# Index lists, row gathers and weight loads of the second expert issued behind a transpose; six constant products ahead of the fold

## The chip, the core and the metric

The kernel runs on one core of one Trainium2 chip. The metric is device time in microseconds, the median of repeated runs. Engines in the text: TensorE (PE, matrix products; its weight loads are PEld), VectorE (DVE), ScalarE (ACT), GpSimd (POOL) and SyncE (SP). SP and POOL here mostly issue DMA transfers; SP issues in the order in which the program is written.

## The reference

Three stages in a row, all in float32.

1. A linear attention with decaying state: for each of 4 batches and 8 heads, 768 steps, `y[t] = r[t] (state + u k[t] v[t])`, then `state = w[t] state + k[t] v[t]`, head size 48.
2. A dense layer on the 3072 rows of 384 values: `h = (x w1 * x w2) w3`, then `x = h w_out` (1024 wide inside).
3. A mixture of 8 experts: a gate `x w_gate` with noise scaled by `log(1 + exp(x w_noise))`, the two highest experts of each row, a softmax over those two, and `out[rows of e] += weight * (max(x[rows of e] w1[e], 0) w2[e])`, 384 to 1024 to 384.

## The kernel before

Nearly every product is done as three products of a high part and a low part (`mm3`, lines 179 to 182: high by high, low by high, high by low), so TensorE's work stands in lines L180, L181 and L182 for all stages.

**Fold.** The first 50 us load `w3` and `w_out`, convert them, and multiply them together once (`mm_w3`), so that stage 2 needs one product less for each row. Lines 529 to 548 are the loop over 19 steps `u`: step `u` converts a piece, `mm_w3(u - 3)` uses the piece of three steps before, `wo_T(u)` transposes a piece of `w_out` on TensorE and `gate_cols(u - 1)` multiplies the piece transposed a step earlier by the gate's weights. `warm_up(n)` (lines 514 to 516) issues `n` products of a constant tile of ones, 128 by 512 in bf16, into a bank that nobody reads; each is pinned behind the TensorE instruction written before it. There are ten before the loop, and three at the end of steps 0 and 1.

**Middle.** Attention, the dense layer and the gate run interleaved from about 50 to 460 us, by a table of slots. The gate writes, for each expert, a list of row numbers and weights into a table in DRAM (`slots`).

**Experts.** An expert has room for 800 rows (CAP), as 7 pieces: pieces 0 to 3 of 128 rows (first half), pieces 4 and 5 of 128 and piece 6 of 32 rows (second half, 288 rows). For each expert the rows come this way:

- `load_idx`: SP loads the list of row numbers from the table (L800; L808 for the first expert).
- `gather`: POOL issues an indirect DMA for each piece, from the rows in DRAM to a tile `xg` (L848; L817 for the first expert).
- `store` (L854; L822 for the first expert): SP writes the piece back to DRAM, in order (`expert_rows`).
- `turn` / `turn_first` (L860, L829): SP issues a DMA transpose from there into `XTx`, which has to wait for the stores.
- `tr` (L865, L866): ACT and DVE make the high and the low part.
- `mm1(hf, ff)`: eight blocks of 9 products into the hidden layer, for one half of the rows. `mm2(e, j)`: the products of piece `j` with the second weights, after which ACT scales the result (L898) and POOL adds it to the output by an indirect DMA (L908).

An expert's weights come as two loads of 768 KB for the first matrix (`load_e(e, 0, i)`, tile `raww`, L781) and two for the second (`load_e(e, 1, i)`, tile `raw`); `split_e` makes their high and low parts (L788, L791).

What sets the order around the change: SP's loads, stores and transposes and the casts of `tr` and `split_e` on ACT are pinned in the order of the program. DVE's order is the program's. POOL's and most of TensorE's instructions are ordered by a planner that goes by its own estimate of when their inputs are there, ties in the order of the program. So SP is one line in which a waiting instruction holds up all behind it.

The first expert is handled apart (lines 1023 to 1072), since its last rows are known only when the gate has ended. The last two pieces of its rows, 5 and 6, are gathered while `mm2` of pieces 0 to 3 already runs (lines 1043 to 1056): after `mm2(0, 0)` come the second expert's first index list and gathers (`need(1, 0, 0)`), the stores of pieces 5 and 6, their transpose (`turn_first(NT - 2, CAP)`, 160 rows, called the late rows below) and the second expert's two first loads. `mm1(1, ff)` of the first expert needs that transpose. Behind its eight blocks the program writes `turn(1, 0)`, which stores and transposes the second expert's first 512 rows. `turn` has an argument `mid`, called between the stores and the transpose; it is used at line 1070 with `load_w2`.

Of the kernel before, what the change touches and what calls it, by code (L numbers as in the profile page):

```python
# [71 lines left out]
def tile_kernel(ctx: ExitStack, tc: tile.TileContext, dt, nat, w3t, wout, w1, w2, e1, e2, cf, ci, out):  # L72
# [63 lines left out]
    def split(h, l, src, on=None):  # L136
        act.copy(out=h, in_=src)
        (on or dve).tensor_tensor(out=l, in0=src, in1=f(h), op=OP.subtract)
# [20 lines left out]
    def flush(n=2):  # L159
        for _ in range(n):  # L160
            low, LQ[:] = LQ[:], []
            while CQ:
                mid, t, z, h, l, post = CQ.pop()
                dve.scalar_tensor_tensor(z, mid, 13, t, op0=OP.logical_shift_right, op1=OP.bitwise_or)
                x = z.bitcast(F32)
                act.copy(out=h, in_=x)
                LQ.append((h, l, x))
                if post:
                    post(x)
            for h, l, x in low:  # L170
                dve.tensor_tensor(out=l, in0=x, in1=f(h), op=OP.subtract)
# [215 lines left out]
    def ld_raw(n=1):  # L387
        for _ in range(n):
            if order:
                k, u = order.pop(0)  # L390
                rawx[k, u] = load64(raws.tile([P, 1026], I32, name="rawf"),
                                    wout[u] if k == "o" else w3t[u // 8, u % 8])

    def cv_wo(j):
        cvt(rawx["o", j], DM, woh[:, j, :DM], wol[:, j, :DM], post=lambda x: xo_.__setitem__(j, x))

    def wo_T(j):
        bank = PB[4 + j % 2]
        for kb in range(3):
            pe.transpose(bank[:, P * kb:P * kb + P], xo_[j][:, kb * P:kb * P + P], ident)  # L400
        xo_[j] = fold.tile([P, DM], F32, name="woT")
        act.copy(out=xo_[j], in_=bank[:, :DM])

    def gate_cols(j):
        g = bK[:, 256 + 32 * j:272 + 32 * j]
        for kb in range(3):
            pe.matmul(g, xo_[j][:, P * kb:P * kb + P], wgn[:, kb], start=kb == 0, stop=kb == 2)

    def gate_split(j):
        split(woh[:, j, DM:], wol[:, j, DM:], bK[:, 256 + 32 * j:272 + 32 * j])  # L410

    def cv_w3(u):
        w3s[u] = [fold.tile([P, 512], F32R, name=x, bufs=3) for x in ("w3h", "w3l")]
        cvt(rawx["3", u], 512, *w3s[u])

    def mm_w3(u):
        jb = u % 8
        for fb in range(4):
            s = slice(fb * P, fb * P + P)
            mm3(PB[fb][:, :XW], w3s[u][0][:, s], w3s[u][1][:, s], woh[:, jb, :], wol[:, jb, :], jb == 0, jb == 7,  # L420
                tc.keep_in_program_order if u == 15 else lambda x: x)
            if u == 7:
                split(W0[0][:, fb], W0[1][:, fb], PB[fb][:, :XW])
# [40 lines left out]
    def run_todo(lo, hi):  # L464
        for slot in sorted(x for x in todo if lo <= x < hi):
            for fn, a in todo.pop(slot):
                fn(*a)
# [46 lines left out]
    def warm_up(n):  # L514
        for _ in range(n):
            tc.keep_in_program_order(pe.matmul(PB[6], warm[:, :P], warm, start=True, stop=True))
# [12 lines left out]
    for u in range(19):  # L529
        if u < 8:  # L530
            cv_wo(u)
            ld_raw()
        if u < 16:
            cv_w3(u)
            ld_raw()
        elif u == 16:
            flush()
        if u > 2:
            mm_w3(u - 3)
        if 0 < u < 9:  # L540
            gate_cols(u - 1)
            gate_split(u - 1)
        if u < 8:
            wo_T(u)
        if u < 2:
            warm_up(3)
        act.on = u >= 15
        run_todo(u - 24, u - 23)
# [226 lines left out]
    def load_e(e, m, i):  # L775
        if m == 0 and e:
            rw = EP["b"].tile([P, 1536], F32, name="raww", bufs=2)
        else:
            rw = rawp.tile([P, 1538], F32, name="raw2", tag="raw64")[:, :1536]
        RW[e, m, i] = rw  # L780
        tc.keep_in_program_order(sp.dma_start(out=rw, in_=(e1, e2)[m][e, :, 1536 * i:1536 * i + 1536]))  # L781
# [11 lines left out]
    def load_idx(e, hf, r):  # L793
        TI[e, hf] = EP["a"].tile([P, (TA, TB + 1)[hf], 2], I32, name=f"ti{hf}", bufs=3)
        for o, n, w, j in (((0, TA, TPT, 0),), ((HOLD, TB, TPT, 0), (CAP - TPL, 1, TPL, TB)))[hf]:
            if isinstance(r, int):
                v = table[e * CAPT + r * CAP + o:e * CAPT + r * CAP + o + w * n]
            else:
                v = table[bass.ds(r * CAP + (e * CAPT + o), w * n)]
            tc.keep_in_program_order(sp.dma_start(out=TI[e, hf][:w, j:j + n].rearrange("p j t -> p (j t)"),  # L800
                                                  in_=v.rearrange("(p j) t -> p (j t)", p=w)))
# [18 lines left out]
    def store_first(j):  # L820
        w = rows_of(j)
        tc.keep_in_program_order(sp.dma_start(  # L822
            out=rows[0, 2 * TPT * j:2 * TPT * j + 2 * w].rearrange("(p t) d -> p (t d)", t=2), in_=XG[0, j][:w]))
# [15 lines left out]
    def rows_of(j):  # L839
        return TPT if j < NT - 1 else TPL  # L840
# [5 lines left out]
    def gather(e, j, rows=NROW):  # L846
        XG[e, j] = EP["b" if e else "a"].tile([P, 2 * DM], U16, name="xg", bufs=NXG)
        pool.indirect_dma_start(out=XG[e, j][:rows_of(j)], out_offset=None, in_=x2d[:rows],  # L848
                                in_offset=bass.IndirectOffsetOnAxis(ap=ti(e, j)[:, 0:1], axis=0))

    def turn(e, hf, mid=lambda: None):

        for j in range(TA) if hf == 0 else range(TA, NT):
            tc.keep_in_program_order(sp.dma_start(  # L854
                out=rows[e % 2, 2 * TPT * j:2 * TPT * j + 2 * rows_of(j)].rearrange("(p t) d -> p (t d)", t=2),
                in_=XG[e, j][:rows_of(j)]))
        mid()
        a = 2 * hf * NAB[0]
        s = slice(a, a + 2 * NAB[hf])
        tc.keep_in_program_order(sp.dma_start_transpose(out=XT["x", hf].bitcast(U16), in_=rows[e % 2, s]))  # L860
# [24 lines left out]
    def mm2(e, j, mid=None):  # L885
        hf, jj = divmod(j, TA)
        n, s = rows_of(j), slice(TPT * jj, TPT * jj + rows_of(j))
        MC[0] ^= 1
        bank = bX[MC[0]][:, :DM]
        y = EP["b"].tile([P, DM], F32, name="ye", bufs=9)  # L890
        wt = ti(e, j)[:, 1:2].bitcast(F32)
        if j < NT - 1:
            for ff in range(8):
                if mid and ff == 4:
                    mid()
                w = slice(ff * DM, ff * DM + DM)
                mm3(bank[:n], Hh[hf][:, ff, s], Hl[hf][:, ff, s], WBh[:, w], WBl[:, w], ff == 0, ff == 7)
            act.activation(out=y[:n], in_=bank[:n], func=AF.Copy, scale=wt)  # L898
        else:

            for ff in range(8):
                g = ff % 4
                pe.matmul(bank[n * g:n * g + n], HM[hf][:, ff], RW[e, 1, ff // 4][:, g * DM:g * DM + DM],  # L903
                          start=ff < 4, stop=ff > 3, tile_position=(0, n * g))
            act.activation(out=y[:n], in_=bank[:n], func=AF.Copy, scale=wt)
            for g in range(1, 4):
                dve.scalar_tensor_tensor(y[:n], bank[n * g:n * g + n], wt, y[:n], op0=OP.mult, op1=OP.add)
        ins = pool.indirect_dma_start(out=out, out_offset=bass.IndirectOffsetOnAxis(ap=ti(e, j)[:, 0:1], axis=0),  # L908
                                      in_=y[:n], in_offset=None, compute_op=OP.add).ins

        if j == 0 or AD[0] != e:
            AD[:] = [e]
        for p in AD[1:]:
            tc.declare_no_dep(ins, p, reason="an expert's rows differ")
        AD.append(ins)

    def need(e, hf, r, rows=NROW):
        load_idx(e, hf, r)
        for j in range(TA) if hf == 0 else range(TA, NT):
            gather(e, j, rows)  # L920
# [125 lines left out]
    for j in range(TA):  # L1046
        mm2(0, j)
        if j == 0:
            need(1, 0, 0)
            for jj in (NT - 2, NT - 1):  # L1050
                store_first(jj)
            turn_first(NT - 2, CAP)
            load_e(1, 0, 0)
            load_e(1, 0, 1)
        if j == TA - 2:
            tr(0, 1)
    need(1, 1, 0)

    def load_w2():
        load_e(1, 1, 0)  # L1060
# [1 line left out]

    for ff in range(8):
        mm1(1, ff)
    turn(1, 0)
    for i, j in enumerate((TA, NT - 1, *range(TA + 1, NT - 1))):
        mm2(0, j)
        split_e(1, 0, i)
# [132 lines left out]
```

## Time and profile before

| what | value |
|---|---|
| median of 3 runs | 903.72 us (902.86 to 906.01) |
| the profiled execution's own time | 909.49 us |
| its span, first to last instruction | 907.7 us |
| PE, PEld | 97%, 90% of the span busy |
| DVE, ACT, POOL | 54%, 48%, 27% |
| mean granted TensorE clock | 0.993 of full speed |
| DMA | 139.18 MB, mean 153 GB/s |
| chain that ended last | PE 41%; DMA 1%, of which the transposes into XTx are the largest part |

Engine shares are shares of the span in which the engine had an instruction running. The granted clock is 1.00 at 2.4 GHz and 0.50 at 1.2 GHz. The chain that ended last is followed back from the last instruction, at each step to what released it. DMA shares are the mean busy share of 16 DMA engines; overlapping packets can bring a stretch above 1.

### The profile page before, as it was taken

How to read it: one execution, taken by the hardware profiler on the slowest of the kernel's cores; microseconds unless marked ns; L12 is line 12 of the kernel's file. 1: busy time of each engine (PE TensorE's matmuls, PEld its weight loads, DVE VectorE, ACT ScalarE, POOL GpSimd, SP SyncE). 2: the span in 40 equal slices, each digit the busy share in tenths (PEclk: the TensorE clock that was granted, in tenths of full speed). 3: DMA queues.
4: the chain of work that ended last, by engine and by line, in shares of the span. 5: the costliest groups of instructions: out<-in, count | busy, mean ns of one | idle time of the engine just before them, and what ended most of it. 6: DMA issues, size and time to landing. Idle time of an engine off the chain costs nothing. (4 is left out here: it accounts for less than half of the span.)

```text
span 907.7 us, 17628 instructions
## 1 busy us (share of the span) xinstructions
PE 882.4 (97%) x7010; PEld 816.1 (90%) x7010; DVE 491.6 (54%) x1208; ACT 436.3 (48%) x883; POOL 242.9 (27%) x216
## 2 busy tenths in 40 slices
PE   8899999999999999999998999999999999999994
PEld 6789799999999999999988989899998989989894
DVE  5899766756666657655472453443434334353430
ACT  7787666555546547544552443433334343433320
POOL 1200010231231231132334443316061341603122
PEclk9999999999999999999999999999999999999997
DMA  9963479474575654515145986829276482934112
GB/s 352 409 232 129 130 99 262 130 196 142 144 216 139 178 134 128 146 44 167 36 114 108 256 249 173 204 73 222 62 214 143 133 213 65 229 76 108 18 21 38
DMA packets 123581, 139.18 MB, mean 153 GB/s; under 512 B 74592, under 2 KB 103264, under 8 KB 123488
## 3 DMA queue, kind: packets, MB, share of 16 engines
q1 hardware_dynamic: 99952, 109.58, 41.3%
q0 software_dynamic: 12160, 19.72, 11.2%
q10 hardware_dynamic: 11376, 8.65, 3.3%
q8 instruction: 57, 0.93, 0.4%
q14 instruction: 36, 0.29, 0.1%
HBM read 88.12 MB, written 36.04 MB: 137 GB/s over the span
## 5 line engine op out<-in xcount | busy, mean ns | idle before, releaser
L908 POOL DMA_INDIRECT out<-ye,ti x49 | 77.4, 1579 | 235.5 <-ACT ye L898 215.3
L180 PE MATMUL pb<-XTh,WAh 128*128 128x512 f32 (+1 forms) x384 | 134.2, 350 | 3.0 <-ACT XTh L865 2.3
L181 PE MATMUL pb<-XTl,WAh 128*128 128x512 f32 (+1 forms) x384 | 133.0, 347 | 0.0
L182 PE MATMUL pb<-XTh,WAl 128*128 128x512 f32 (+1 forms) x384 | 131.8, 347 | 0.0
L180 PE MATMUL pb<-WBh,HH 128*128 128x384 f32 x384 | 130.2, 339 | 0.0
L181 PE MATMUL pb<-WBl,HH 128*128 128x384 f32 x384 | 129.3, 337 | 0.0
L182 PE MATMUL pb<-WBh,HH 128*128 128x384 f32 x384 | 129.3, 337 | 0.0
L881 DVE SCALAR_TENSOR_TENSOR HH<-pb,HH 128x256 fp32r<-128x256 f32 (+1 forms) x128 | 71.3, 557 | 87.2 <-ACT HH L880 79.9
L880 ACT ACTIVATE HH<-pb 128x256 fp32r<-128x256 f32 (+1 forms) x128 | 62.8, 491 | 115.2 <-PE pb L182 108.2
L898 ACT ACTIVATE ye<-pb,ti 128x384 f32<-128x384 f32 x42 | 24.4, 581 | 134.0 <-PE pb L182 108.4
L725 POOL DMA_INDIRECT slots<-g_sc,g_si x48 | 51.9, 1081 | 136.9 <-DVE g_si L724 71.9
L180 PEld LDWEIGHTS pb<-XTh,WAh 128*128 128x128 f32 x384 | 72.7, 189 | 15.1 <-DVE HH L881 4.0
L180 PE MATMUL pb<-xh,WAh 128*128 128x256 f32 x288 | 82.0, 285 | 0.3 <-ACT xh L86 0.3
L180 PE MATMUL pb<-xh,WBh 128*128 128x256 f32 x288 | 81.5, 283 | 0.0
L181 PE MATMUL pb<-xl,WAh 128*128 128x256 f32 x288 | 81.0, 282 | 0.2 <-DVE xl L337 0.2
L181 PE MATMUL pb<-xl,WBh 128*128 128x256 f32 x288 | 81.0, 281 | 0.0
L182 PE MATMUL pb<-xh,WAl 128*128 128x256 f32 x288 | 81.0, 282 | 0.0
L182 PE MATMUL pb<-xh,WBl 128*128 128x256 f32 x288 | 81.0, 281 | 0.0
L181 PEld LDWEIGHTS pb<-XTl,WAh 128*128 128x128 f32 x384 | 72.8, 190 | 8.8 <-DVE XTl L866 0.3
L182 PEld LDWEIGHTS pb<-XTh,WAl 128*128 128x128 f32 x384 | 72.3, 189 | 8.8 <-DVE WAl L791 0.2
L180 PEld LDWEIGHTS pb<-WBh,HH 128*128 128x128 f32 x384 | 72.1, 188 | 5.0 <-ACT WAh L788 3.8
L241 POOL TENSOR_TENSOR rku<-nrk 128x384 f32<-128x384 f32 x21 | 21.6, 1028 | 198.7 <-DVE cc L248 83.5
(194 smaller groups left out, 2063.5 us busy)
## 6 DMA issues: line engine op xcount, KB each, us to landing
dtc<-dt SPq DMA_DIRECT2D x24, 772.0 KB
raw<-e SPq DMA_DIRECT2D x18, 768.0 KB
raww<-e SPq DMA_DIRECT2D x14, 768.0 KB
nrk<-nat SPq DMA_DIRECT2D x24, 384.0 KB
expert_rows<-xg SPq DMA_DIRECT2D x45, 192.0 KB
rawf<-w3t SPq DMA_DIRECT2D x16, 512.0 KB
nv<-nat SPq DMA_DIRECT2D x24, 256.0 KB
out<-zeros SPq DMA_DIRECT2D x9, 576.0 KB
```

Source lines behind the costliest of these rows:

```text
L180: pin(pe.matmul(o, wh, xh, start=start, stop=False))
L181: pe.matmul(o, wh, xl, start=False, stop=False)
L182: pe.matmul(o, wl, xh, start=False, stop=stop)
L241: on.tensor_tensor(out=t, in0=RK[j][:, :DM], in1=RK[j][:, DM:], op=OP.mult)
L725: ins = pool.indirect_dma_start(out=table, out_offset=bass.IndirectOffsetOnAxis(ap=si[:, i, k:k + 1], axis=0), in_=SC[:, i, k, :], in_offs ...
L880: act.activation(out=Hh[hf][:, ff], in_=bank[:, :n], func=AF.Relu)
L881: dve.scalar_tensor_tensor(Hl[hf][:, ff], bank[:, :n], 0.0, f(Hh[hf][:, ff]), op0=OP.max, op1=OP.subtract)
L898: act.activation(out=y[:n], in_=bank[:n], func=AF.Copy, scale=wt)
L908: ins = pool.indirect_dma_start(out=out, out_offset=bass.IndirectOffsetOnAxis(ap=ti(e, j)[:, 0:1], axis=0), in_=y[:n], in_offset=None, com ...
```

## The change

In the fold, the three constant products at the end of step 1 go, and six stand in step 1 between `gate_split(0)` and `wo_T(1)`. Step 0 keeps its three.

In the first expert, `need(1, 0, 0)` (one index list on SP, four gathers on POOL) moves from ahead of the stores of pieces 5 and 6 to behind the issue of their transpose. The second expert's two loads of its first weights move from behind that transpose into `turn(1, 0, load_w1)`: on SP they then stand behind the index list of the second half (`need(1, 1, 0)`) and the four stores of the second expert's first 512 rows, and ahead of the transpose of these rows.

```diff
         if 0 < u < 9:
             gate_cols(u - 1)
             gate_split(u - 1)
+        if u == 1:
+            warm_up(6)
         if u < 8:
             wo_T(u)
-        if u < 2:
+        if u == 0:
             warm_up(3)
...
     for j in range(TA):
         mm2(0, j)
         if j == 0:
-            need(1, 0, 0)
             for jj in (NT - 2, NT - 1):
                 store_first(jj)
             turn_first(NT - 2, CAP)
-            load_e(1, 0, 0)
-            load_e(1, 0, 1)
+            need(1, 0, 0)
         if j == TA - 2:
             tr(0, 1)
     need(1, 1, 0)
 
+    def load_w1():
+        load_e(1, 0, 0)
+        load_e(1, 0, 1)
+
     def load_w2():
...
     for ff in range(8):
         mm1(1, ff)
-    turn(1, 0)
+    turn(1, 0, load_w1)
```

## Rows read from the trace of the kernel before

**Rows 1.** Page, part 1: busy us, share of the span, instructions of each engine.
```profile
PE 882.4 (97%) x7010; PEld 816.1 (90%) x7010; DVE 491.6 (54%) x1208; ACT 436.3 (48%) x883; POOL 242.9 (27%) x216
```

**Rows 2.** PE's waits from 500 us on: us in total, times, longest.
```profile
PE pb L180 <- DVE HH L881: 0.3, 1, 0.3
```

**Rows 3.** Chain that ended last, 485 to 500.5 us: start, us, what.
```profile
485.54 3.05 DMA xg<-x_rows,tf
...
491.95 6.61 DMA XTx<-expert_rows
```

**Rows 4.** PE in order of time, 499 to 521 us: start, us, what, idle before.
```profile
499.06 0.55 PE L180 MATMUL pb<-XTh,WAh 128*128 128x288 f32 x1 [2.27 <-ACT XTh L865]
...
520.34 0.40 PE L180 MATMUL pb<-XTh,WAh 128*128 128x512 f32 x1
```

**Rows 5.** SP's issues in order of time, 450 to 518 us: start, us of issuing, what.
```profile
453.64 1.21 SPq L829 DMA_TRANSPOSE XTx<-expert_rows  x1
...
475.27 1.21 SPq L829 DMA_TRANSPOSE XTx<-expert_rows  x1
...
483.04 0.42 SPq L800 DMA_DIRECT2D ti<-slots  x1
488.61 1.17 SPq L822 DMA_DIRECT2D expert_rows<-xg  x2
491.95 1.27 SPq L829 DMA_TRANSPOSE XTx<-expert_rows  x1
493.26 1.05 SPq L781 DMA_DIRECT2D raww<-e  x2
494.36 0.90 SPq L800 DMA_DIRECT2D ti<-slots  x2
...
506.31 4.18 SPq L860 DMA_TRANSPOSE XTx<-expert_rows  x1
```

**Rows 6.** POOL in order of time, 484 to 516 us.
```profile
487.09 0.88 POOL L817 DMA_INDIRECT xg<-x_rows,tf  x1 [0.58 <-DMA ti<-slots]
488.28 0.96 POOL L848 DMA_INDIRECT xg<-x_rows,ti  x1 [0.30 <-issue]
...
493.30 1.64 POOL L908 DMA_INDIRECT out<-ye,tf  x1 [0.30 <-issue]
...
504.70 1.01 POOL L848 DMA_INDIRECT xg<-x_rows,ti  x1 [7.89 <-DMA ti<-slots]
```

**Rows 7.** Stretches of the expert stage: engines' busy us, PE clock, DMA share, GB/s.
```profile
454.50:456.00 1.50, 1.50 (x15) 1.50 (x14) 1.14 (x11) 0.59 (x2) 0.00 (x0) 1.00 0.62 130
477.50:480.00 2.50, 2.50 (x13) 2.00 (x12) 2.44 (x6) 1.32 (x2) 0.67 (x1) 1.00 0.57 68
...
494.00:496.50 2.50, 2.50 (x17) 2.47 (x15) 0.00 (x0) 0.00 (x0) 2.20 (x2) 1.00 1.25 97
498.50:503.00 4.50, 3.94 (x17) 3.68 (x18) 1.72 (x5) 1.96 (x5) 0.00 (x0) 0.62 1.09 333
499.10:502.60 3.50, 3.50 (x14) 3.24 (x15) 1.45 (x4) 1.44 (x4) 0.00 (x0) 0.51 1.05 327
539.00:542.50 3.50, 3.50 (x27) 3.31 (x26) 1.86 (x6) 1.77 (x4) 0.00 (x0) 1.00 1.18 280
```

**Rows 8.** ACT in order of time, 498 to 521 us.
```profile
515.23 0.82 ACT L788 CAST WAh<-raww 128x768 fp32r<-128x768 f32 x1
...
517.44 1.65 ACT L865 CAST XTh<-XTx 128x512 fp32r<-128x512 f32 x3
```

**Rows 9.** PE in order of time, 6 to 11 us.
```profile
6.06 0.81 PE L516 MATMUL pb<-warm 128*128 128x512 bf16 x3
...
8.88 0.63 PE L180 MATMUL pb<-WBh,w3h 128*128 128x400 f32 x2 [1.25 <-ACT w3h L166]
```

**Rows 10.** Stretches of the fold, columns as in rows 7.
```profile
8.90:20.00 11.10, 10.68 (x67) 9.78 (x67) 8.40 (x18) 9.06 (x20) 0.29 (x1) 1.00 1.03 412
20.00:35.00 15.00, 13.29 (x81) 11.56 (x82) 11.86 (x24) 10.46 (x23) 2.21 (x2) 1.00 1.03 404
```

## The prediction

> **What bounds the kernel now.** The page's first part comes first: TensorE is busy 97% of the span [rows 1], so what an edit is worth is the TensorE idle time that it takes away, plus time at a low clock. TensorE's waits from 500 us on come to 0.3 us in all [rows 2]: behind the first expert's stage TensorE runs without a gap to the end, so a microsecond won or lost by about 500 us arrives at the end whole. Then TensorE in order of time: the largest gap of the run is 2.27 us ahead of 499.06, ended by the cast of `XTh` [rows 4]. The chain of waits says what that cast stood for: the transpose of the late rows, issued at 491.95, 6.61 us [rows 3]. Last, the stretches: from 499.1 to 502.6 the granted clock is 0.51, the 1.2 GHz level, with TensorE busy all through [rows 7]. That half speed came right behind the gap and costs 3.5 x 0.49 = 1.7 us. The gap and the half speed, 2.27 + 1.7 = 4.0 us, are what the expert part of the change can win at most.
>
> **The change part by part.**
>
> *What leaves the late rows' transpose.* Beside it now run four gathers, issued from 488.28 to 493.3 on POOL [rows 6], each 128 rows of 1536 bytes, 0.79 MB together, and behind it on SP two loads of 768 KB from 493.26 [rows 5]. From 494 to 496.5 the DMA engines are full (1.25) and move only 97 GB/s [rows 7]. The transpose could take, for its 160 rows:
> - 6.61 us if what leaves never mattered (upper end: gain nil);
> - about 5.3 us by the transpose issued at 475.27 [rows 5]: 128 rows, whose bytes still move up to 480 [rows 7], 4.7 us, with a few row writes of the table beside it, plus some for 160 rows;
> - about 3.1 us by the one issued at 453.64 [rows 5], with nothing ahead of it: 130 GB/s x 1.5 us = 0.195 MB by 456 [rows 7], which is all of its 128 rows, so 2.4 us to the last byte.
>
> I take 4.0 us, nearest to the quiet one: 2.4 MB leave, and the scatter-adds of the first expert's results stay beside it (POOL comes to them sooner, since the gathers no longer stand ahead of 493.30). Stores and issue stay where they are, 491.95. Landing is then 495.95, the cast takes some 0.5 us, and the last product ahead of the gap ends at 499.06 - 2.27 = 496.79. So the gap goes (gain 2.27). With 5.3 us the landing is 497.25, TensorE starts at 497.75, a gap of 1.0 (gain 1.3). The 1.25 us gap ahead of 8.88 [rows 9] left the clock at 1.00 in the stretch behind it [rows 10], so below such a gap I count the half speed as gone too (1.7). Gain here: 4.0 taken, 3.0 by the middle row, 0 to 4.0 as bounds.
>
> *A rule on what shares the engines.* The trace has a tiny index load issued from 494.36 behind two weight loads on SP [rows 5], whose gather could start only at 504.70 [rows 6]. The Trainium skill (DMA: Bandwidth & Descriptors, Queues, rings and completion order) has each DMA engine consume one issuer's descriptors in ring order and take turns between issuers by packets; the index load agrees. By that rule the two weight loads behind the transpose never slowed it, only POOL's gathers did. The sum for the first edit is then the gathers' alone, still between the bounds above; and loads put ahead of a transpose hold it up in full, which is how I count them next.
>
> *What becomes late next: the second expert's first rows.* Before, their transpose is issued at 506.31 [rows 5], it has landed when its cast runs at 517.44 [rows 8], and TensorE reaches the second expert at 520.34 [rows 4]; with 4.0 us won, at 516.3. The moved steps, in SP's new order: the index list follows the late rows' transpose, at 491.95 + 1.27 = 493.2. It took 4.05 us before (483.04 [rows 5] to POOL's release at 487.09 [rows 6]), and can't pass the transpose: gathers from 497.2 instead of 488.28. Four of them at (493.30 - 488.28) / 4 = 1.25 us: the last starts at 501.0 and lands after 3.05 [rows 3], 504.0. Its store, then the two loads (1.05 us of issuing), meanwhile the store lands after some 2.2 us (489.78 to 491.95 for the first expert's, [rows 5]): the transpose's issue at 506.4, as before, because before the stores stood behind the loads. But now the loads are ahead of it: 1.57 MB at 333 GB/s [rows 7] is 4.7 us, from about 505.2 to 509.9; then 512 rows, 0.79 MB at 280 GB/s or a little better (539 to 542.5, the same transpose one expert on, [rows 7]), 3 to 3.5 us, and a landing of 0.4: 513.8. The first of three casts is 0.6 (1.65 for three, [rows 8]): TensorE could start at 514.4, against 516.3. Cover 1.9 us; gone, each further microsecond costs one, and a gap like the present one another 1.7 of clock. The weights' first cast, at 515.23 before [rows 8], comes to 511.2 and its load is there at about 508: no loss.
>
> *Six constant products.* Three take 0.81 us [rows 9], six at most 1.62, into the 1.25 us in which TensorE waits for `w3h`: the first fold product comes up to 0.4 us later, and the three products that stood behind `wo_T(1)` give 0.8 back. From 8.9 to 35 us the DMA engines are full (1.03) at over 400 GB/s while TensorE idles 0.4 and 1.7 us [rows 10]: the fold goes at the pace of its loads, and what TensorE wins or loses within 0.4 us is hidden there. I take 0. Bounds: 0.4 us lost if nothing hid it, 0.4 won; and 1.7 won in an execution whose clock, unlike this one's, falls in that gap.
>
> **Sum.** 909.49 - 4.0 = 905.5 for a profiled execution. The median of runs stands 5.8 below the profiled execution's 909.49; carried over: 903.72 - 4.0 = 899.7, and I forecast 899.8.
>
> **The rivals.**
>
> *A. As worked out.* Gap and half speed go, nothing is late: 899.8 (3.0 to 4.3 won, 900.7 to 899.4). Chance 0.45.
>
> *B. The stall is smaller, or goes by half.* The three runs lie 3.15 us apart, about the size of the stall with its clock, and the profiled execution is the slowest of all; runs without the profiler may have the gap and the half speed only sometimes. Or the transpose stays at 5.3 us or more and the clock still falls. About 2.0 won: 901.7. Chance 0.25.
>
> *C. Nothing in sum.* The late rows' transpose is slow by itself, as at 475.27, where little ran beside it; or POOL takes the scatter-adds of pieces 2 and 3 ahead of the four gathers, 1.94 us each [rows 6], so that the second expert's rows land 3.9 later, at 517.7: TensorE starts at 518.3, a 2.0 us gap, perhaps 1.7 of clock, and 0.3 is left of 4.0. Time 903.5. Chance 0.15. Against it: the gathers are written ahead of those scatter-adds, and their inputs are ready sooner.
>
> *D. Slower: the second expert's rows become the new stall.* The index list now stands behind a transpose as the one issued from 494.36 stood behind loads; that one's gather started 10.3 us later (504.70), 6.3 more than the 4.05 counted. Then the transpose lands at 520.1, TensorE starts at 520.7 where it should at 516.3: 4.4 of gap and 1.7 of clock against 4.0 won, 2.1 slower. With the loads at 97 to 187 GB/s as around 494 in place of 333, 1 to 4 us more. Time about 906.3. It decides from the point at which the rows come 4.2 us later than worked out (1.9 of cover, then 2.3 of gap with 1.7 of clock). Against it: the list before waited for 1.5 MB, here for 0.25 MB. Chance 0.15.
>
> **How the numbers follow.** What a measurement of this kernel can tell from no change is about 0.3%, 2.7 us: 901.0 and 906.4. Faster: most of A (0.41) and a third of B (0.08), 0.49. Slower: most of D, with runs from 906.4 on, 0.11, and 0.01 of C. Same: the rest, 0.40. Range: 898.6 takes in A with some 1.2 us more for the fold's clock; 905.4 takes in B, C and the start of D, leaving out about 0.12 of D and 0.05 below.
>
> **What would show it.** Right: in the trace after, no gap of over 1 us ahead of the first expert's `mm1(1, .)`, clock 1.00 there, the transpose at 3 to 5 us in the chain, TensorE reaching the second expert about 4 us sooner without a gap, and unchanged waits for `w3h`. The second expert's gathers should start at 496 to 498 and its transpose land at 513 to 515. Wrong: a wait of TensorE for `XTh` of 128x512 at about 516 to 520 (C or D), or the same 2 us gap with gathers and loads gone from beside it (then the transpose was slow by itself). If the gap is gone and the median hasn't moved, the stall was one of the profiled execution (B).

## The result, and the profile after

The changed kernel takes **909.48 us** (median of 11 runs, 906.72 to 914.62), the kernel before 903.72 (11 runs beside them, 902.71 to 908.13). The ratio is 1.0061 [1.0044, 1.0077]: slower by 0.6%. Rival D had said 906.3, the forecast was 899.8. The profiled execution took 911.50 us (span 909.7) against 909.49. Three runs of the experiments are over 1.5% above the fastest of their kernel (921.19 us in g1, 1727.01 in g3, 1072.38 in g4), and ratios and clock counts, though not medians, are taken without them.

TensorE, VectorE and the rest do the work they did [rows 1]. Part 1 of the page after: busy us, share of the span, instructions of each engine.

```profile
PE 883.1 (97%) x7013; PEld 818.6 (90%) x7013; DVE 492.9 (54%) x1208; ACT 436.6 (48%) x883; POOL 242.7 (27%) x216
```

After 500 us TensorE used to wait 0.3 us in all [rows 2]. TensorE's waits after, same stretch: us in total, times, longest.

```profile
PE pb L180 <- ACT XTh L867: 5.9, 1, 5.9
```

(Lines of this kernel stand two below those of before: L867 is the cast of the transposed rows, L862 the transpose, L910 the scatter-add.) TensorE in order of time: start, us, what, idle before in brackets.

```profile
509.75 1.50 PE L905 MATMUL pb<-raw,HM 128*32 128x384 f32 x16
...
515.34 0.34 PE L182 MATMUL pb<-WBh,HH 128*128 128x384 f32 x1
521.54 0.79 PE L180 MATMUL pb<-XTh,WAh 128*128 128x512 f32 x1 [5.87 <-ACT XTh L867]
...
554.79 1.50 PE L905 MATMUL pb<-raw,HM 128*32 128x384 f32 x16
```

The same view of the kernel before: the x16 row is the first, then the second expert's short last piece.

```profile
514.64 1.50 PE L903 MATMUL pb<-raw,HM 128*32 128x384 f32 x16
...
551.91 1.50 PE L903 MATMUL pb<-raw,HM 128*32 128x384 f32 x16
```

At the first expert's short last piece the changed kernel is 4.9 us ahead (514.64 - 509.75); at the second's it is 2.9 behind. So 7.8 us were lost in between. TensorE has nothing to do from 515.67 to 521.54, and then the clock is low. Stretches after, columns as in [rows 7]:

```profile
503.40:507.30 3.90, 3.90 (x29) 3.90 (x28) 1.57 (x6) 1.05 (x3) 2.91 (x2) 1.00 0.98 334
507.30:520.90 13.60, 8.38 (x55) 6.79 (x53) 3.66 (x5) 2.62 (x5) 3.39 (x2) 0.92 1.25 163
518.80:525.60 6.80, 4.06 (x9) 2.94 (x10) 3.73 (x5) 3.59 (x6) 1.57 (x1) 0.50 1.08 340
```

From 518.8 to 525.6 the granted clock is 0.50, the 1.2 GHz level; 4.06 us of it are busy, so 2.0 are lost: 5.87 + 2.0 = 7.9, the 7.8 found. What ended the wait stands in the chain of waits after (start, us, what), and SP's issues and POOL's work say what ran beside it.

```profile
503.39 17.46 DMA XTx<-expert_rows
...
520.87 0.63 ACT XTh L867
```

SP's issues after (start, us of issuing, what):

```profile
487.89 1.27 SPq L831 DMA_TRANSPOSE XTx<-expert_rows  x1
489.21 1.51 SPq L802 DMA_DIRECT2D ti<-slots  x3
495.38 4.76 SPq L856 DMA_DIRECT2D expert_rows<-xg  x4
500.18 0.98 SPq L783 DMA_DIRECT2D raww<-e  x2
503.39 11.60 SPq L862 DMA_TRANSPOSE XTx<-expert_rows  x1
```

POOL after (start, us, what, idle before):

```profile
492.29 0.98 POOL L850 DMA_INDIRECT xg<-x_rows,ti  x1 [5.54 <-DMA ti<-slots]
...
496.18 0.95 POOL L850 DMA_INDIRECT xg<-x_rows,ti  x1 [0.30 <-issue]
...
503.08 1.65 POOL L910 DMA_INDIRECT out<-ye,tf  x1 [0.30 <-issue]
505.04 1.58 POOL L910 DMA_INDIRECT out<-ye,tf  x1 [0.31 <-ACT HH L882]
510.71 1.56 POOL L910 DMA_INDIRECT out<-ye,tf  x1 [4.09 <-ACT ye L900]
514.37 1.83 POOL L910 DMA_INDIRECT out<-ye,tf  x1 [2.09 <-DVE ye L909]
```

The late rows' transpose, 6.61 us before [rows 3], lands 3.2 us after its issue at 487.89, and no wait for it is left. The gathers start at 492.29 at distances of 1.3 us. But the second expert's transpose, issued at 503.39 and so 2.9 us earlier than before [rows 5], takes 17.46 us. For the first 3.9 us the DMA engines move mostly the two weight loads put ahead of it (334 GB/s); for 13.6 us after that they are full (1.25) and move 163 GB/s, with scatter-adds from POOL beside the transpose. It moves 3072 packets of 256 bytes. Their median is 18 ns, but some take far longer: the means of each 2 us or so in those 13.6 us stand between 33 and 118 ns, where the same transpose one expert on has 18 to 20 in the kernel before, with nothing from POOL beside it. (Times of packets and of landings that no view prints are the trace's own records of packets and completions.)

In the fold, the gap of 1.25 us [rows 9] is filled, and what [rows 10] showed at full clock is not all at full clock here. TensorE, then a stretch, after:

```profile
7.81 1.46 PE L516 MATMUL pb<-warm 128*128 128x512 bf16 x6
9.22 0.63 PE L180 MATMUL pb<-WBh,w3h 128*128 128x400 f32 x2
```

```profile
27.30:30.70 3.40, 3.40 (x13) 3.25 (x13) 2.37 (x5) 1.47 (x3) 0.00 (x0) 0.50 1.02 408
```

### The profile page after: what moved, and what is told of

Its sections match the earlier page's. It is cut to its first block, busy times and chain, and to the rows that moved or that the text cites. A ratio compares the mean times of both kernels' runs of the same rounds, so it can differ in the third digit from the quotient of the medians.

```text
span 909.7 us, 17633 instructions
## 1 busy us (share of the span) xinstructions
PE 883.1 (97%) x7013; PEld 818.6 (90%) x7013; DVE 492.9 (54%) x1208; ACT 436.6 (48%) x883; POOL 242.7 (27%) x216
## 4 chain that ended last, share of the span: by engine, by line
PE 86%; DVE 6%; DMA 3%; ACT 2%; issue 1%; POOL 0%; POOLq 0%; SPq 0%; ACTq 0%
PE pb L180 26%; PE pb L181 25%; PE pb L182 25%; PE pb L330 3%; PE pb L261 2%; DMA XTx<-expert_rows 2%; PE pb L905 1%; PE pb L293 1%; DVE cvz L164 1%; DMA rawf<-w3t 1%; PE pb L516 1%; DVE fg L208 1%; DMA rawf<-w 0%; DVE am L266 0%; PE pb L407 0%
## 5 line engine op out<-in xcount | busy, mean ns | idle before, releaser
L910 POOL DMA_INDIRECT out<-ye,ti x49 | 77.4, 1579 | 231.7 <-ACT ye L900 208.6
```

## The experiments

Each ratio is to the kernel before, run beside it on the same chip; it is not simply the quotient of the two medians. The runs e, f and g were made on three chips, whose medians for the kernel before are 905.39, 911.82 and 913.09 us; which chip gave the first result is not on record. Diffs are against the kernel before where nothing else is said. First come four parts of the change (one chip), then what stands behind them.

**e1, the six products alone.**

```diff
+        if u == 1:
+            warm_up(6)
         if u < 8:
             wo_T(u)
-        if u < 2:
+        if u == 0:
             warm_up(3)
```

> The six constant products alone, expert stage as before. Theory 1 (the fold pays part of the loss): in the profile after, the fold ran 3.4 us at half clock from 27.3 us and the first attention products stood 1.4 to 1.6 us later than before, so 0.9 to 1.6 us slower than before, a half-speed stretch at about 27 us again. Rival (that half-speed stretch was one execution's chance and the fold goes at the pace of its loads): within 0.4 us of before, clock 1.00 from the first warm stretch to the expert stage in some executions of either kernel.

Measured: 902.80, ratio 0.9972 [0.9955, 0.9990]: 0.3% faster. Two findings. First, the mean granted clock is 0.994 to 0.996 in all 12 runs, where 11 of 29 runs of the kernel before have 0.993 or less. In the profiles each stretch at 1.2 GHz of 3.4 us costs 1.7 us and takes 0.0019 off the mean clock (the idle last 9 to 12 us are low in all of them); every profile at 0.993 or less has one or more before that end. e1's profile has none in the fold, but neither has the profile of the kernel before, and TensorE does as much there (stretch 8 to 110 us, before and e1, columns as in [rows 7]):

```profile
8.00:110.00 102.00, 95.55 (x834) 85.28 (x835) 88.87 (x175) 75.35 (x168) 4.93 (x5) 1.00 0.67 251
8.00:110.00 102.00, 95.73 (x832) 84.80 (x829) 89.92 (x174) 75.40 (x168) 5.17 (x5) 1.00 0.67 251
```

Second, its expert stage is the one of before, gathers ahead of the late rows' transpose and all, and there is no wait: TensorE's waits from 485 to 560 us give no row. The transfers issued from 489 to 494 (KB each, median us to landing) and the cast that the 6.61 us had held up, on ACT:

```profile
XTx<-expert_rows SPq DMA_TRANSPOSE x1, 4.3
```

```profile
493.65 1.10 ACT L867 CAST XTh<-XTx 128x288 fp32r<-128x288 f32 x3 [0.72 <-DMA XTx<-expert_rows]
```

The same transpose takes 4.3 us and is in time. The stall is not a property of the kernel but of some of its executions.

**e2, the expert part alone** (all of the second hunk of the change, the fold as before).

> The expert part of the change alone, fold as before. Theory 1 (most of the loss is the new stall on the second expert's rows): about 4 us slower than before, a TensorE gap of 4 to 6 us ahead of the second expert's first product with 3 to 7 us at half clock behind it, no gap ahead of the first expert's second half. Rival (the loss is the fold's): within 1 us of before or faster.

Measured: 909.91 (six runs), 1.0056 [1.0035, 1.0077]. The loss is here. SP, TensorE and two stretches:

```profile
504.13 9.40 SPq L860 DMA_TRANSPOSE XTx<-expert_rows  x1
```

```profile
518.27 0.50 PE L180 MATMUL pb<-XTh,WAh 128*128 128x512 f32 x1 [3.71 <-ACT XTh L865]
```

```profile
507.70:517.60 9.90, 6.87 (x46) 5.28 (x44) 3.66 (x5) 2.60 (x4) 3.39 (x2) 1.00 1.26 177
...
519.80:523.20 3.40, 3.40 (x10) 2.63 (x9) 2.17 (x3) 1.40 (x2) 1.57 (x1) 0.51 1.06 306
```

The transpose takes 13.45 us from issue to landing: a gap of 3.71 and 3.4 us at half speed, 5.4 lost.

**e3, the gathers late, the loads not ahead of the second transpose.**

```diff
-            need(1, 0, 0)
...
             turn_first(NT - 2, CAP)
+            need(1, 0, 0)
             load_e(1, 0, 0)
             load_e(1, 0, 1)
```

> Fold as before; the index list and the four gathers stand behind the late rows' transpose as in the change, but the two weight loads follow the index list at once instead of standing between stores and transpose. Theory 1 (the loads ahead of the transpose of the second expert's rows make it late): the late rows' transpose stays at about 3 us and the gap ahead of it goes, the second expert's transpose is issued later than before but has nothing of the loads left ahead of it; 2 to 4 us faster than before. Rival a (the gathers are late by themselves, and slow down the transpose beside which they and the scatter-adds run): a gap of 2 to 5 us ahead of the second expert remains, 0 to 3 us slower. Rival b (the loads now delay the second half's index list and the stores, as before): gathers on time, stores land behind the loads at 503 to 505, gain 2 to 3.

Measured: 904.07, 0.9994 [0.9979, 1.0010]. SP and the stretch over the transpose:

```profile
490.56 0.89 SPq L781 DMA_DIRECT2D raww<-e  x2
...
504.30 4.77 SPq L860 DMA_TRANSPOSE XTx<-expert_rows  x1
```

```profile
504.30:512.40 8.10, 8.10 (x58) 6.84 (x57) 2.20 (x7) 2.70 (x6) 3.71 (x3) 1.00 1.12 202
```

8.1 us and no wait. That the gathers move back is harmless by itself: the transpose is issued at 504.30, as in e2 (504.13).

**e4, the loads ahead of the second transpose, the gathers where they were.**

```diff
-            load_e(1, 0, 0)
-            load_e(1, 0, 1)
...
-    turn(1, 0)
+    turn(1, 0, load_w1)
```

> Fold as before; the gathers stay where they were, only the two weight loads move in between the stores and the transpose of the second expert's rows. Theory 1 (loads ahead of a transpose hold it up): the late rows' transpose still stands beside the gathers, 5 to 6.6 us, gap of 1 to 2 us as before; the second expert's rows are stored by about 499, so their loads and transpose start some 5 us sooner than in the changed kernel and the rows come at about 512 to 515: no second gap, 0 to 1.5 us faster than before. Rival (loads ahead of the transpose are what makes it slow, however early): a gap of 2 us or more ahead of the second expert, 2 to 5 us slower.

Measured: 905.25, 0.9994 [0.9978, 1.0010]. SP, and the transfers issued from 498 to 513:

```profile
495.11 0.94 SPq L781 DMA_DIRECT2D raww<-e  x2
498.18 6.99 SPq L860 DMA_TRANSPOSE XTx<-expert_rows  x1
```

```profile
XTx<-expert_rows SPq DMA_TRANSPOSE x1, 13.3
```

With loads ahead the transpose takes 13.3 us here too, but it is issued 6 us earlier and lands at 511.5, before TensorE wants it. So of the two moves each is hidden alone, and together they are not: the loads make the transpose longer (13.3 against 8.1 to 11.5 in the profiles of before, e1, f4, g1 and g4, whose gathers stand early too), and the late gathers take away the 6 us in which that would not show.

**f1, the kernel before, profiled once more** on the second chip.

> The kernel before, unchanged, for one more profiled execution. Theory 1 (the 2.27 us stall on the late rows with its half speed belonged to that one profiled execution, in which the transposes at 475 and 492 us were slow): the late rows' transpose lands 3.5 to 5 us after its issue and there is no gap of over 0.5 us ahead of the first expert's second half, as in the profile with the fold alone, whose expert stage is the same. Rival (the stall is the rule and the other profile was the exception): again a gap of 1.5 to 2.5 us with 3.4 us at half clock behind it.

Measured: 912.43 (one run). The stall is there again, 6.51 us of transpose and 2.19 of gap, but the half speed behind it is not (TensorE, then the stretch behind the gap):

```profile
499.97 0.40 PE L180 MATMUL pb<-XTh,WAh 128*128 128x288 f32 x1 [2.19 <-ACT XTh L865]
```

```profile
500.00:503.50 3.50, 3.40 (x24) 3.19 (x25) 1.73 (x6) 1.83 (x5) 0.00 (x0) 1.00 1.06 324
```

**f2, the loads behind the second transpose** (the expert part, with `turn(1, 0)` and then `load_w1()`).

> Fold as before; expert stage as in the change, but the two weight loads are issued behind the transpose of the second expert's rows instead of ahead of it. Theory 1 (the loads ahead of it on the same queue are what makes that transpose 13 to 17 us long): it lands 7 to 9 us after an issue at 503 to 505, at 511 to 513, so no gap for the rows; the loads start at about 508 and come at 513 to 516, so the casts of the weights may hold up the second expert by up to 2 us: within 2 us of before, 3 to 5 us faster than the expert part alone. Rival (the traffic of GpSimd's queue beside it makes it long): still 12 us or more, gap of 3 us or more, 4 to 6 us slower than before.

Measured: 915.52, 1.0045 [1.0020, 1.0070]. SP, ACT and TensorE:

```profile
505.80 4.40 SPq L860 DMA_TRANSPOSE XTx<-expert_rows  x1
510.25 1.04 SPq L781 DMA_DIRECT2D raww<-e  x2
```

```profile
517.45 0.82 ACT L788 CAST WAh<-raww 128x768 fp32r<-128x768 f32 x1
518.18 1.65 ACT L865 CAST XTh<-XTx 128x512 fp32r<-128x512 f32 x3
```

```profile
521.52 0.50 PE L181 MATMUL pb<-XTl,WAh 128*128 128x512 f32 x1 [1.44 <-DVE XTl L866]
```

The transpose lands by 514.5, 8.7 us after its issue at the latest. Now the weights are late: their casts run up to 518.2, the rows' cast waits its turn on ACT behind them, and the rows' remainder `XTl` on VectorE behind the weights' remainder, 1.44 us too late. Another gap of 1.62 us, from 506.75 on, waits for `HM`, which this edit doesn't move, and it stays unexplained. The profile is of the fastest of the ten runs (911.59 us, clock 0.996, about the median of the kernel before); the other nine have clocks of 0.987 to 0.993. So the 0.45% goes with time at 1.2 GHz in executions of which no profile was taken, and where that falls is not shown.

**f3, the expert part without the first expert's scatter-adds.**

```diff
+        if e == 0:
+            return
```

(ahead of the indirect DMA in `mm2`, besides all of e2's diff)

> Fold as before; expert stage as in the change, but the first expert's results are not added to the output (its seven scatter-adds are left out). Theory 1 (loads ahead make the transpose long): the transpose of the second expert's rows still begins to move only when the loads are through and lands 10 to 12 us after its issue at 502 to 504; gap of 0 to 2 us. Rival (the scatter-adds beside it make it long: its packets took 34 to 143 ns in the changed kernel while scatter-adds ran, 18 to 20 ns elsewhere): it lands 8 to 9 us after its issue with the loads still ahead of it, no gap, 4 to 6 us faster than the expert part alone.

Measured: 911.63, 0.9999 [0.9971, 1.0026]. SP, then the stretch of the loads, issued at 508.48, and the one of the transpose:

```profile
512.79 6.41 SPq L860 DMA_TRANSPOSE XTx<-expert_rows  x1
```

```profile
512.80:515.50 2.70, 2.70 (x13) 2.70 (x13) 0.52 (x2) 0.38 (x1) 0.00 (x0) 0.54 0.97 359
515.50:521.20 5.70, 5.70 (x41) 4.43 (x41) 0.62 (x3) 1.68 (x3) 0.00 (x0) 1.00 1.23 207
```

With the loads ahead and nothing from POOL the transpose takes 8.4 us: 2.7 for the loads, 5.7 for itself. No wait for the rows is left, but that alone says little: a 2.2 us wait for `HM`, with the half speed seen in the first row behind it, is this profile's own and gave the rows some 3.9 us. Without it they would have been about 0.3 us late (an estimate: landed at 521.2, 0.6 for the first cast, against the 525.36 at which TensorE came to them, less 3.9). What counts is the 8.4 us, against 13.3 to 17.5 in the four profiles with loads ahead and scatter-adds beside (e2, e4 and g3, on other chips, and the change).

The same transpose with neither stands in every profile: the third expert's first rows, which have no loads ahead and nothing from POOL beside them. In e2 (SP, then the transfers issued from 537 to 543):

```profile
537.66 3.04 SPq L860 DMA_TRANSPOSE XTx<-expert_rows  x1
```

```profile
XTx<-expert_rows SPq DMA_TRANSPOSE x1, 5.1
```

Over the 14 profiles it took 5.1 to 6.0 us from issue to landing.

**f4, three products in the gap in place of six** (the three of step 1 are moved from behind `wo_T(1)` to ahead of it).

> Expert stage as before; in the fold the three products of step 1 stand in front of the transpose of the second piece as in the change, but they stay three. Theory (the six products help because they fill the 1.25 us gap at about 8 us, behind which the clock falls to half speed in some executions, 1.7 us each): three fill 0.6 us of it, a gap of about 0.6 us is left, and the mean clock of the runs is as with six, 0.994 to 0.996: 1.5 to 2.5 us faster than before. Rival (the number of products matters, so that the clock is held up by what is issued as a whole): the runs' clocks spread from 0.990 to 0.996 as before's do and the time is within 1 us of before.

Measured: 909.73, 0.9969 [0.9942, 0.9995]. The gap ahead of the fold is 0.60 us instead of 1.25; 4 of 12 runs have a clock of 0.993 or less, of the kernel before 14 of 29. The late rows' transpose takes 5.6 us by the chain and TensorE waits 0.44 for it. The second expert's transpose, with no loads ahead of it, takes 11.5 us (SP, then the cast that waits for it):

```profile
504.77 5.91 SPq L862 DMA_TRANSPOSE XTx<-expert_rows  x1
```

```profile
516.31 1.66 ACT L867 CAST XTh<-XTx 128x512 fp32r<-128x512 f32 x3 [1.47 <-DMA XTx<-expert_rows]
```

**g1, six products behind `wo_T(1)`**: twice the warm-up, none of it in the gap.

```diff
-            warm_up(3)
+            warm_up(6 if u else 3)
```

> Expert stage as before; in the fold six products at the end of step 1, where three stood, so that only their number is as in the change and the gap ahead of the fold stays. Theory (what helps is that products stand inside the 1.25 us gap at about 8 us): the gap stays, the clocks of the runs spread as before's do, time within 1 us of before or up to 1 us slower. Rival (the number helps, wherever they stand): 1.5 to 2.5 us faster than before, mean clocks of 0.994 or more in nearly all runs.

Measured: 911.92, 0.9987 [0.9952, 1.0022]; 6 of 11 runs at 0.993 or less (before: 21 of 35). TensorE, then a stretch of the fold:

```profile
9.47 0.64 PE L180 MATMUL pb<-WBh,w3h 128*128 128x400 f32 x2 [1.26 <-ACT w3h L166]
```

```profile
27.50:31.00 3.50, 3.50 (x13) 3.40 (x13) 2.41 (x6) 1.74 (x4) 0.00 (x0) 0.51 1.02 409
```

The gap stays, and there is a stretch at half speed, but the profile of the change has one at the same place with the gap filled. So this doesn't show that it is the place of the products that counts: the runs' clocks speak for it (6 of 11 low here, 4 of 11 with the six ahead of `wo_T(1)` on this chip, g4), the time doesn't (0.9987 here, 0.9988 in g4).

**g2, the six products and e3's expert stage**: the version that the experiments point to.

> The six products as in the change, the index list and gathers behind the late rows' transpose as in the change, but the two loads right behind the index list instead of between the second expert's stores and transpose. Theory 1 (the fold part wins about 2.5 us; the late rows' transpose at 3 us in place of 4 to 6.6 takes away a stall of about 2 us that about half of the executions have; and without the loads ahead of it the second expert's transpose is on time): 2.5 to 4 us faster than before, at least as fast as the fold part alone. Rival (the two parts don't add, as they did not in the change): 1.5 us or less faster, slower than the fold part alone.

Measured: 908.77, 0.9965 [0.9943, 0.9987], the lowest median on its chip; the clock is 0.995 or 0.996 in 11 of 12 runs. The second expert's transpose, issued at 506.63, lands 7.8 us later by the one completion on record, and TensorE doesn't wait for it.

**g3 and g4, the change and e1 again**, on the third chip.

> The whole change once more, beside the fold part alone on the same chip. Theory 1 (the expert part costs 5 to 6 us, the fold part wins 2.5): 2.5 to 6 us slower than before, 5 to 8 slower than the fold part alone, with a gap of 3 to 6 us ahead of the second expert. Rival (the fold part loses when the expert part is there): 7 us or more slower than before.

> The six products alone once more, for a comparison on the same chip. Theory 1: 2 to 3 us faster than before, mean clocks of 0.994 or more. Rival (the first result was that chip's): within 1 us of before.

Measured: g3 915.61, 1.0035 [0.9997, 1.0074]; g4 910.53, 0.9988 [0.9960, 1.0016], with 4 of 11 runs at 0.993 or less. Neither interval excludes no change by itself. g3's profile repeats the mechanism (chain, then TensorE):

```profile
511.58 15.32 DMA XTx<-expert_rows
```

```profile
527.59 0.79 PE L180 MATMUL pb<-XTh,WAh 128*128 128x512 f32 x1 [6.48 <-ACT XTh L867]
```

## Why the prediction was wrong

**The gain of 4.0 us: the mechanism was right, the price was one execution's.** Gap 2.27 and half speed 1.7 were read from one profile and carried over in full to the median. Seven profiles of this work have the gathers ahead of the late rows' transpose: it took 6.5 to 6.6 us in two of them (before, f1), 5.6 in f4, about 5.4 in g1 and g4, 4.3 and 4.9 in e1 and e4. TensorE waited 2.2 us in two, 0.4 in one and not at all in four; the half speed followed once. With the gathers behind it, seven profiles have 2.9 to 3.3 us and never a wait. So the edit does what was worked out, even a little better than the 4.0 taken, but it mostly shortens a transfer that is hidden anyway: e3, which has this gain and no loss, is 0.9994. Rival B named this, and I gave it 0.25. The sign against the 4.0 stood in the times: 909.49 was the slowest of the runs shown.

**The second expert's rows: the term that was mis-sized.** I wrote: issue at 506.4, 4.7 us of loads from 505.2, 3 to 3.5 of transpose, 0.4 of landing, so 7.4 from issue to landing and 1.9 of cover. Measured from issue to landing: 13.45 (e2), 15.32 (g3), 17.46 (the change). The issue was even 2.3 (e2) and 3.0 us (the change) earlier than worked out. The terms:

- Loads ahead: 3.5 counted behind the issue, 2.7 (f3) to 3.9 us (the change). About right.
- The transpose itself and its landing: 3 to 3.5 and 0.4 counted, the first by the rate of another stretch [rows 7], the second from no row. For that other transpose, the third expert's at 537.53, both hold: 1.3 us from issue to first packet, 3.4 of packets, 0.5 to the landing. This one doesn't run alone. In the trace of before, with nothing ahead of it on SP, it landed 8.4 us after its issue at 506.31: 1.6 to the first packet, 4.1 of packets, 2.7 from the last of them to the landing. No view prints that landing, but it was in the trace to be read. With 4.1 + 2.7 behind the loads the sum is 516.7 for the rows and 517.3 with the cast, past the 516.3 at which TensorE wanted them: a small gap, on the way to rival D, in place of 1.9 us of cover.
- What runs beside it: left out, and this is the step that failed. I put "the scatter-adds of the first expert's results stay beside it" on the late rows' side only, where they cost nothing. In the runs with the loss the packets alone took 8.0 (e2), 10.0 (g3) and 12.3 us (the change), and the landing 0.9 to 1.8.

The transposes of the same 512 rows, from issue to landing, can be set side by side. With neither loads ahead nor POOL beside: 5.1 to 6.0 (the third expert's, 14 profiles). With loads ahead alone: 8.4 (f3). With POOL's transfers beside it alone: 8.1 and 8.7 with the gathers late, as in the change (e3, f2), and 8.1 to 11.5 in the order of before (before, e1, f4, g1, g4). With both: 13.3 (e4), 13.5 (e2), 15.3 (g3), 17.5 (the change). With the gathers late, each alone adds 2 to 3.6 us to the undisturbed transpose, which would make 10.5 to 12 in sum; with both it is 13.5 to 17.5.

A figure of the Trainium skill (DMA: Bandwidth & Descriptors, Latency and other measured facts) prices the moving and not the neighbours: its 261 GB/s for a DMA transpose would give an estimate of 3.0 us for 0.79 MB. The 3.4 us of packets in the undisturbed transpose come near it; the 8.0 to 12.3 us do not.

The explanation that f3 bears out is that the loads push the transpose back into a stretch in which POOL's scatter-adds (four from 503.08 to 514.37 after) share full DMA engines with it. Why the two together cost more than their sum is not shown. The Trainium skill (DMA: Bandwidth & Descriptors, Queues, rings and completion order) says that a DMA engine takes one issuer's work in order and changes between issuers packet by packet; the first half agrees with e2 against f2 (13.45 with loads ahead, 8.7 with loads behind), and the second fits f3. By the order alone, on which I leaned, the rows would have been in time.

**Rival D's place was right and its cause was not.** It had the index list late; the list came 3.1 us after its issue (489.21 to 492.29), sooner than the 4.05 counted. The late step was the transpose.

**The six products: 0 was wrong, the bound's mechanism was right.** e1 wins 0.28% (2.6 us) on one chip, f4 0.31% on another, g2 0.35% with e3's neutral stage on the third; g4's 0.12% [-0.16%, 0.40%] there doesn't contradict it. The gain goes with the clock, but that they win by filling the gap is likely and not shown (g1). I had read "clock 1.00 behind the gap" [rows 10] from one execution; in others the fold drops to 1.2 GHz, at 8.8 to 12.2 and 43.0 to 46.4 us in e4, twice 1.7 us and so more than the bound. Such a stretch stands in the fold in four of the eight profiles with the gap open (e3, e4, f3, g1) and in one of the six with it filled or nearly so: the profile of the change has 3.4 us at 0.50 from 27.3. Only in e4 and f3 does one start within 1 us of the gap's end.

**The sum.** e1 and e2 multiply to 0.9972 x 1.0056 = 1.0028; the change measured 1.0061 [1.0044, 1.0077] at first and 1.0035 [0.9997, 1.0074] on the chip of g. The second agrees, the first is above the product. Part of it may be that the gap differs between executions: 3.7 us in e2, 5.9 and 6.5 in the two profiles of the change; this is not shown. Also open: why the late rows' transpose differs by 2 us between executions of one order of work, and the waits of up to 2.2 us for `HM` and `HH` in most profiles of the runs f and g.

## What to carry to other kernels

A stall seen in one profile is not yet a price, and even a second profile that shows it (f1) does not make it one: count it by the share of executions that have it (here 2 of 7). Two moves that are each hidden alone can use up the same cover: sum the delay of both against the one step that needs the data. When a transfer is pushed back, take its duration from its own landing in the trace, and look at which transfers of other issuers run at its new place.

## What the runs showed of the hardware

- A DMA transpose of 512 rows (0.79 MB, in 256-byte packets) took 5.1 to 6.0 us from issue to landing with nothing beside it, 8.4 with two loads of 768 KB ahead of it, 8.1 to 11.5 with POOL's transfers beside it, 13.3 to 17.5 with both. SP was held while issuing it: 3.0 us in quiet (e2, at 537.66), 3.1 to 6.9 with POOL's transfers beside it (e1, g4 among others), 6.4 to 11.6 with loads ahead (f3, the change), so that everything behind it on SP came later as well.
- The same gap of TensorE, 2.27 and 2.19 us at the same place, was followed by 3.5 us at 1.2 GHz in one execution and by full clock in the other. Behind a gap of 1.25 us, ahead of the fold, the clock stayed at 1.00 in before and was 0.50 for 3.4 us in e4.
- Six products of 1.46 us in all, in a gap of 1.25, went with a lower share of runs whose mean granted clock is 0.993 or less: 0 of 12 against 11 of 29 (e1) and 1 of 12 against 21 of 35 (g2); but g4, the same kernel as e1 on the chip of g2, has 4 of 11.
